# An attention and feed-forward kernel on one core: W_out's staging in a pool of its own, and three kinds of instruction in another place

## The chip, the cores and the metric

One core of a Trainium2 chip runs the whole program. Five engines work beside each other, each with its own list of instructions that it takes in order: TensorE (PE, with its weight loads as PEld), VectorE (DVE), ScalarE (ACT), GpSimd (POOL) and SyncE (SP), which issues the transfers. The metric is the device time of one execution in microseconds, the median of several.

## The reference

Eight batches of eight heads with 576 positions of 64 features go through attention with a block-causal mask (blocks of 64), then all 4608 tokens through a feed-forward layer with 512 in, 2048 hidden and 512 out.

```python
scores = scale * np.matmul(q, k.transpose(0, 1, 3, 2))      # scale = 1/8
scores = np.where(block_i >= block_j, scores, -1e9)
scores = scores - np.max(scores, axis=-1, keepdims=True)
attn = np.exp(scores)
attn = attn / (np.sum(attn, axis=-1, keepdims=True) + 1e-09)
x = np.matmul(attn, v)                                      # to (4608, 512)
h = x @ w_in
return ((h / (1 + np.exp(-h))) @ w_out).astype(np.float32)
```

## The kernel before, in words

The first two query blocks of each head are treated by special code at the start (`First`, `Second`). The other 448 query positions of each head are the main loop: 64 heads, called units u0 to u63, taken as 32 pairs d0 to d31, the even head in the upper half of the array's rows and the odd head in the lower half. The order of everything is written out by hand: `ORDER` is a long string of tokens such as `u36.max:0`, and the loop at L1258 calls the named method for each token. What a token emits goes to the end of its engine's list, so the table sets the order on each engine, and an engine waits at an instruction whose input is late.

For one pair, the steps are these.

- `dN.run:0` and `dN.run:1` (L793, matmuls at L802) are two runs of matmuls. Run 0 interleaves the scores of the even head with half of the product with v of the pair two earlier (tile `U`); run 1 does the same for the odd head (tile `u`). Scores lie in three PSUM banks for each head: x, y and z (names `S`, `S` and `SC` for the even head, `S`, `S` and `U` for the odd one).
- `max:0..2` (DVE, L663) takes block maxima of z, x and y into `Mx`; `ones` (ACT, L719) moves some of them across partitions; the end of `max:2` reduces them to `mj` (L715). `gather` (three ACT copies, L672), `top` (DVE, L727 and L729), `spread` (three ACT copies, L733) and `wide` (DVE, L667) bring the maximum of each row to where it is subtracted (`MR`). `sub:0..2` (DVE, L741 and L744) read the scores out of PSUM, which frees the banks, and `exp:0..2` (ACT, L748) follow.
- `add:0..3` (POOL, L755 to L763) add up the exponentials into `pa`, and `sums` (DVE, L663, tile `dj`) makes the row sums of it, once for each head. `sums_g` (three ACT copies), `sums_m` (POOL, L818 to L822) and `inverse` (DVE, L826 and L667) make the reciprocals.
- `half` (ACT, L806) and `fold` (DVE, L809) bring the product with v together, `mult` (POOL, L831) multiplies with the reciprocals, `x_hi` (ACT, L836) and `x_lo` (POOL, L839) split the result into two parts for the feed-forward layer.

The first feed-forward matmuls fill PE between the runs: each token `ffn` is six matmuls (L1077), two tokens fill a bank `h`, `keep` (ACT, L1083) copies it out to SBUF, which frees the bank, and `save` (SP) stores it to DRAM. There are two such banks, and the product `u` of each pair takes its turn in them too. Most pairs have eight `ffn` (48 matmuls of 448 columns); the pairs d2 to d5 and d9 have six (d2 to d4 with 512 columns, d5 with half of each).

Beside this, W_out is staged: 16 row blocks `o0` to `o15`, two for each of `t0` to `t7`. `load` brings 512 KB (tile `wst`), `rebias` (ACT, L540) and `bits:0..2` (DVE, L563, L567, L573) turn the 64-bit numbers into 32-bit ones in the tile `wraw`, and `hi` (ACT), `lo` and `x` (POOL for t0 to t3) make the split parts and differences for the second layer. t0 to t3 go into the pool `ta`, and t4 to t6 into a pool that exists only after the token `all.attended`, which releases the loop's pool:

```python
def attended(u):
    pools["work"].release()
    pools["work"] = tc.alloc_tile_pool(name="end", bufs=1, reuse_waits="tile")
```

The tiles of the staging (`os0`, `os1`, `wraw`) come from `pools["work"]` too, so those of before the token and those of behind it are different tiles. Behind the token stand o8 to o15, 42 `ffn` without attention, and then the second layer (items i0 to i71, L1160), which runs to the end.

Of the kernel before, what the change touches and what calls it, by code (L numbers as in the profile page):

```python
# [101 lines left out]
u1.exp:2 save u0.add:1 ffn u1.sub:1 u1.exp:0 u0.add:2 o2.bits:1 u1.exp:1 u0.add:3 o2.bits:2 d1.run:0 keep u1.add:0 u0.sums
o3.rebias save o3.bits:0 u1.add:1 o3.bits:1 u1.add:2 ffn u6.load u2.max:0 u7.load u1.add:3 u2.max:1 u2.ones ffn u2.max:2
u3.max:0 u2.gather ffn u3.ones u2.top keep u3.max:1 u2.spread u3.max:2 save ffn u2.wide u3.gather u2.sub:0 ffn keep u3.top
u2.sub:1 u3.spread save u1.sums u2.exp:0 ffn u2.sub:2 d0.sums_g u3.wide u2.exp:1 d0.sums_m ffn u3.sub:2 u2.exp:2 keep u3.sub:0
u3.exp:2 u3.sub:1 u2.add:0 save ffn d0.inverse u3.exp:0 u3.exp:1 u2.add:1 o3.bits:2 d2.run:0 keep u2.add:2 t1.hi:0 u2.add:3 save
t1.hi:1 u3.add:0 u2.sums d2.run:1 d0.half u4.max:0 u3.add:1 u4.max:1 u4.ones u3.add:2 u4.max:2 u3.add:3 u4.gather ffn u4.load_v
d0.fold t1.lo:0 u5.load_v u8.load u9.load u5.max:0 u4.top ffn d0.mult u5.ones u5.max:1 u4.spread u5.max:2 t1.lo:1 d0.x_hi ffn
u4.wide keep u4.sub:0 u5.gather d0.x_lo save ffn u4.exp:0 u5.top u4.sub:1 t1.x:0 u5.spread u3.sums ffn u4.exp:1 u4.sub:2 keep
u4.add:0 u5.wide d1.sums_g save ffn u5.sub:2 u4.exp:2 d1.sums_m t1.hi:2 u5.sub:0 u5.exp:2 u5.sub:1 d3.run:0 u4.add:1 keep  # L110
d1.inverse u5.exp:0 save u4.add:2 u5.exp:1 u4.add:3 d3.run:1 u5.add:0 d1.half u4.sums u6.max:0 u5.add:1 u6.max:1 u6.ones
u6.max:2 u5.add:2 ffn u5.add:3 u6.load_v u7.load_v d1.fold u10.load u11.load u6.gather u7.max:0 d1.mult ffn u6.top u7.ones
u7.max:1 u6.spread t1.lo:2 u7.max:2 d1.x_hi ffn u6.wide keep d1.x_lo u7.gather u6.sub:0 save ffn t1.x:1 u7.top u6.exp:0 u6.sub:1
u7.spread u5.sums t1.x:2 ffn u6.exp:1 u6.sub:2 keep u7.wide u6.add:0 d2.sums_g save ffn u7.sub:2 u6.exp:2 d2.sums_m u7.sub:0
u7.exp:2 u7.sub:1 d4.run:0 u7.exp:0 keep u6.add:1 d2.inverse u7.exp:1 save u6.add:2 t1.hi:3 u6.add:3 d4.run:1 d2.half u7.add:0
u6.sums u8.max:0 u7.add:1 u8.max:1 u8.ones u8.max:2 ffn u7.add:2 u8.load_v u9.load_v u12.load u7.add:3 u13.load d2.fold
u8.gather u9.max:0 ffn d2.mult u8.top u9.ones u9.max:1 u8.spread t1.lo:3 u9.max:2 ffn keep u8.wide u9.gather save ffn u8.sub:0
d2.x_hi u9.top u8.exp:0 d2.x_lo u8.sub:1 u9.spread u7.sums ffn keep u8.sub:2 d3.sums_g save u9.wide ffn u8.exp:1 d3.sums_m
u9.sub:2 u8.exp:2 u9.sub:0 u9.exp:2 d5.run:0 u9.sub:1 keep u8.add:0 d3.inverse u9.exp:0 save u9.exp:1 u8.add:1 u8.add:2 d5.run:1
d3.half u8.add:3 u9.add:0 u8.sums u10.max:0 ffn u9.add:1 u10.max:1 u10.load_v u10.ones u11.load_v u14.load u15.load u10.max:2  # L120
u9.add:2 u9.add:3 ffn d3.fold u10.gather u11.max:0 d3.mult u10.top u11.ones ffn u11.max:1 keep u11.max:2 u10.spread save ffn
u11.gather u10.wide d3.x_hi u10.sub:0 d3.x_lo u11.top u10.exp:0 u10.sub:1 u11.spread u9.sums u10.exp:1 ffn u10.sub:2 d4.sums_g
u10.add:0 u11.wide u10.exp:2 ffn u11.sub:2 keep d4.sums_m u11.sub:0 u11.exp:2 save d6.run:0 u11.sub:1 keep u11.exp:0 u10.add:1
save d4.inverse u11.exp:1 u10.add:2 u10.add:3 d6.run:1 d4.half u11.add:0 u10.sums u12.max:0 u11.add:1 u12.max:1 u12.ones ffn
u12.max:2 u11.add:2 u12.load_v u13.load_v u16.load u17.load u11.add:3 d4.fold u12.gather ffn u13.max:0 d4.mult u12.top u13.ones
u13.max:1 ffn u12.spread u13.max:2 keep u12.wide ffn d4.x_hi save u13.gather d4.x_lo u12.sub:0 ffn u13.top keep u12.sub:1
u13.spread save u11.sums ffn u12.exp:0 u12.sub:2 d5.sums_g u13.wide ffn u12.exp:1 d5.sums_m u13.sub:2 keep u13.sub:0 u12.exp:2
save ffn u13.sub:1 u13.exp:0 u12.add:0 d5.inverse u13.exp:1 d7.run:0 u13.exp:2 u12.add:1 keep u12.add:2 save u12.add:3 d7.run:1
u13.add:0 d5.half u12.sums u14.max:0 u13.add:1 u14.max:1 u14.ones u14.max:2 u13.add:2 ffn u13.add:3 u14.load_v u15.load_v
d5.fold u18.load u19.load u14.gather u15.max:0 d5.mult ffn u14.top u15.ones u15.max:1 u14.spread ffn u15.max:2 keep u14.wide  # L130
d5.x_hi save ffn u15.gather d5.x_lo u14.sub:0 u15.top u14.exp:0 ffn u14.sub:1 keep u13.sums u15.spread save u14.sub:2 ffn
d6.sums_g u15.wide u14.exp:1 d6.sums_m u15.sub:2 ffn u14.exp:2 u15.sub:0 keep u15.exp:2 u15.sub:1 u14.add:0 save ffn d6.inverse
u15.exp:0 u15.exp:1 u14.add:1 d8.run:0 keep u14.add:2 save u14.add:3 u15.add:0 u14.sums d8.run:1 d6.half u16.max:0 u15.add:1
u16.max:1 u16.ones u16.max:2 u15.add:2 u15.add:3 ffn u16.gather u16.load_v d6.fold u17.load_v u20.load u21.load u17.max:0
d6.mult ffn u16.top u17.ones u17.max:1 u16.spread u17.max:2 ffn keep u16.wide u17.gather save ffn u16.sub:0 d6.x_hi u17.top
u16.exp:0 d6.x_lo u16.sub:1 ffn u17.spread u15.sums keep u16.sub:2 d7.sums_g ffn save u17.wide u16.exp:1 d7.sums_m u17.sub:2
u16.exp:2 ffn u17.sub:0 keep u17.sub:1 u17.exp:0 u16.add:0 save ffn d7.inverse u17.exp:1 u17.exp:2 u16.add:1 d9.run:0 keep
u16.add:2 save u16.add:3 u17.add:0 u16.sums d9.run:1 d7.half u18.max:0 u17.add:1 u18.max:1 u18.ones u17.add:2 u18.max:2
u17.add:3 u18.gather ffn u18.load_v d7.fold u19.load_v u22.load u23.load u19.max:0 d7.mult ffn u18.top u19.ones u19.max:1
u18.spread u19.max:2 ffn keep u18.wide u19.gather save ffn u18.sub:0 d7.x_hi u19.top u18.exp:0 d7.x_lo u18.sub:1 u19.spread  # L140
u17.sums keep u18.sub:2 ffn d8.sums_g save u19.wide u18.exp:1 d8.sums_m u19.sub:2 ffn u18.exp:2 u19.sub:0 u19.exp:2 u19.sub:1
d10.run:0 u19.exp:0 u18.add:0 d8.inverse keep u19.exp:1 save u18.add:1 u18.add:2 d10.run:1 u18.add:3 d8.half u19.add:0 u18.sums
u20.max:0 u19.add:1 u20.max:1 ffn u20.ones u20.load_v u21.load_v u24.load u25.load u20.max:2 u19.add:2 u19.add:3 ffn d8.fold
u20.gather u21.max:0 d8.mult ffn u20.top u21.ones u21.max:1 keep u21.max:2 u20.spread save ffn d8.x_hi u20.wide u21.gather
d8.x_lo ffn u20.sub:0 keep u21.top u20.exp:0 u20.sub:1 save ffn u21.spread u19.sums u20.sub:2 d9.sums_g ffn u21.wide keep
d9.sums_m u20.exp:1 u21.sub:2 save ffn u20.exp:2 u21.sub:0 u21.exp:2 u20.add:0 u21.sub:1 u21.exp:0 d11.run:0 d9.inverse keep
u20.add:1 u21.exp:1 save u20.add:2 u20.add:3 d11.run:1 d9.half u21.add:0 u20.sums u22.max:0 u21.add:1 u22.max:1 u22.ones
u22.max:2 u21.add:2 ffn u22.load_v u23.load_v u26.load u21.add:3 u27.load d9.fold u22.gather ffn u23.max:0 d9.mult u22.top
u23.ones u23.max:1 ffn u22.spread u23.max:2 keep u22.wide d9.x_hi ffn save u23.gather d9.x_lo u22.sub:0 ffn u23.top u22.exp:0
u22.sub:1 keep u21.sums u23.spread save ffn u22.sub:2 d10.sums_g u23.wide u22.exp:1 ffn d10.sums_m u23.sub:2 keep u22.exp:2  # L150
u23.sub:0 save ffn u23.exp:2 u23.sub:1 u22.add:0 d10.inverse u23.exp:0 u23.exp:1 d12.run:0 u22.add:1 keep u22.add:2 save
u22.add:3 u23.add:0 d12.run:1 u22.sums d10.half u24.max:0 u23.add:1 u24.max:1 u24.ones u24.max:2 u23.add:2 ffn u23.add:3
# [1158 lines left out]
```

## Time and profile before

| | |
|---|---|
| median of 3 runs | 962.75 us (962.7 to 963.15) |
| the profiled execution's own time | 963.81 us |
| its span, first to last instruction | 962.1 us |
| mean granted TensorE clock | 1.000 |
| PE busy / PEld busy | 98% / 86% |
| DVE / ACT / POOL busy | 76% / 67% / 58% |

The profiled execution is some 1.1 us longer than the median of the runs, and 1.7 us of it lie outside the span. Busy shares are over the whole span. The ends of matmuls are modelled, and one overlaps the next, so that a busy PE may still start its matmuls late: starts are what to compare.

### The profile page before, as it was taken

The page shows a single profiled execution, that of the slowest core. Times are in us where ns is not written, and L with a number is a line of the kernel's source. Part 1 is how long each engine was busy: PE and PEld are TensorE (multiplying, and loading weights), DVE is VectorE, ACT ScalarE, POOL GpSimd, SP SyncE. Part 2 cuts the span into 40 slices and gives each one's busy share as a digit, 9 for nine tenths or more (in the row PEclk, how much of TensorE's full clock was granted, in tenths as well). Part 3 has the DMA queues.
Part 4 walks back from the last instruction along what each step waited for, and adds up shares of the span by engine and source line. Part 5 has one row for each costly group of instructions (what it writes and reads, how often), then busy time and mean ns, then how long its engine had stood idle before and what let it go on. Part 6 is the DMA issues. An engine that isn't in the chain of part 4 may idle for free.

```text
span 962.1 us, 23795 instructions
## 1 busy us (share of the span) xinstructions
PE 945.1 (98%) x8730; PEld 823.9 (86%) x8730; DVE 735.1 (76%) x1515; ACT 641.4 (67%) x1621; POOL 558.9 (58%) x803
## 2 busy tenths in 40 slices
...
GB/s 354 389 161 178 117 105 125 124 112 126 133 105 133 116 175 122 105 133 166 115 128 110 89 112 235 201 153 155 154 162 146 111 162 139 139 124 152 143 67 44
DMA packets 109813, 139.97 MB, mean 145 GB/s; under 512 B 22656, under 2 KB 87168, under 8 KB 109696
## 3 DMA queue, kind: packets, MB, share of 16 engines
...
## 4 chain that ended last, share of the span: by engine, by line
PE 46%; DVE 20%; POOL 17%; ACT 8%; issue 5%; DMA 2%; SPq 0%; POOLq 0%; DVEq 0%; ACTq 0%
PE c L1160 20%; PE S L1160 16%; DVE Mx L663 9%; PE h L1077 8%; POOL pa L758 4%; POOL pa L755 4%; POOL pa L763 3%; POOL rs L822 3%; DVE dj L663 2%; ACT m L733 2%; ACT g L1083 2%; DVE MR L667 2%; ACT dj L672 2%; DVE xu L809 2%; DVE p L741 2%
## 5 line engine op out<-in xcount | busy, mean ns | idle before, releaser
L1077 PE MATMUL h<-x,wi 128*128 128x448 f32 (+2 forms) x1968 | 417.5, 368 | 7.9 <-ACT g L1083 4.2
L1077 PEld LDWEIGHTS h<-x,wi 128*128 128x128 f32 x1968 | 356.1, 188 | 53.4 <-ACT g L1083 11.6
L1142 POOL TENSOR_TENSOR wi<-raw,wi 128x512 fp32r<-128x512 f32 (+1 forms) x114 | 115.8, 1031 | 148.6 <-ACT wi L1138 107.9
L748 ACT ACTIVATE p<-p 128x448 f32<-128x448 f32 (+2 forms) x192 | 100.9, 571 | 5.3 <-DVE p L741 1.6
L802 PE MATMUL S<-qk 64*64 64x384 f32 (+1 forms) x512 | 99.2, 517 | 0.0
L1083 ACT COPY g<-h 128x448 f32<-128x448 f32 (+1 forms) x160 | 85.7, 536 | 20.1 <-PE h L1077 14.8
L663 DVE TRANSPOSE_TENSOR_REDUCE dj<-pa 128x14 f32<-128x448 f32 x64 | 40.6, 634 | 73.5 <-POOL pa L763 73.5
L1160 PE MATMUL c<-ta,wi 128*128 128x256 f32 x684 | 87.0, 276 | 0.0
L1105 ACT ACTIVATE raw<-raw 128x1024 f32<-128x1024 f32 x72 | 76.7, 1065 | 13.7 <-DMA raw<-gdb 9.9
L758 POOL TENSOR_TENSOR pa<-pa,p 128x256 f32<-128x256 f32 (+1 forms) x128 | 79.1, 618 | 10.0
L755 POOL TENSOR_TENSOR pa<-p 128x448 f32<-128x448 f32 x64 | 73.2, 1143 | 15.8 <-ACT p L748 10.9
L1160 PEld LDWEIGHTS c<-ta,wi 128*128 128x128 f32 x684 | 81.9, 188 | 0.0
L1160 PE MATMUL c<-tb,wi 128*128 128x256 f32 x498 | 81.4, 276 | 0.0
L802 PE MATMUL U<-p,v 64*64 64x64 f32 (+4 forms) x768 | 79.8, 354 | 0.8 <-DVE p L744 0.8
L719 ACT COPY Mx<-Mx 64x4 f32<-64x4 f32 x128 | 24.7, 193 | 81.4 <-DVE Mx L663 79.8
L802 PE MATMUL u<-p,v 64*64 64x64 f32 (+4 forms) x768 | 78.6, 351 | 0.0
L741 DVE TENSOR_TENSOR p<-S,MR 128x448 f32<-128x448 f32 (+1 forms) x128 | 71.6, 581 | 1.1
L1160 PEld LDWEIGHTS c<-tb,wi 128*128 128x128 f32 x498 | 71.0, 188 | 0.0
L1160 PE MATMUL S<-ta,wi 128*128 128x256 f32 x534 | 70.2, 276 | 0.0
L663 DVE TRANSPOSE_TENSOR_REDUCE Mx<-S 128x14 f32<-128x448 f32 (+1 forms) x128 | 69.2, 576 | 0.0
L802 PEld LDWEIGHTS u<-p,v 64*64 64x64 f32 x768 | 43.9, 133 | 28.2 <-issue 23.2
L1160 PEld LDWEIGHTS S<-ta,wi 128*128 128x128 f32 x534 | 65.0, 188 | 0.0
...
## 6 DMA issues: line engine op xcount, KB each, us to landing
gdb<-g SPq DMA_DIRECT2D x128, 224.0 KB, 1.9
...
```

Of the source, the lines that this page charges most:

```text
L663: nc.vector.tensor_reduce(out=out, in_=in_, axis=AX.X, op=op, apply_transpose=True)
L741: nc.vector.tensor_tensor(out=u.p[:, c : c + w], in0=s[:, :w], in1=u.mb[:, q : q + w], op=ALU.subtract)
L748: nc.scalar.activation(u.p[:, c : c + w], u.p[:, c : c + w], AF.Exp, scale=SCALE)
L755: nc.gpsimd.tensor_tensor(out=u.pa, in0=p[:, :NQ], in1=p[:, ZERO:COLS], op=ALU.add)
L758: nc.gpsimd.tensor_tensor(out=u.pa[:, q : q + w], in0=u.pa[:, q : q + w], in1=p[:, c : c + w], op=ALU.add)
L763: nc.gpsimd.tensor_tensor(out=o, in0=o, in1=s, op=ALU.add)
L802: nc.tensor.matmul(o, w, x, start=start, stop=stop)
L1077: nc.tensor.matmul(o, w, x, start=half == 0 and i == 0 or f is None and i == 0, stop=(half == 1 or f is None) and i == len(runs) - 1)
L1083: nc.scalar.copy(g, hs.pop(z)[:, :n])
L1105: nc.scalar.activation(u.raw, u.raw, AF.Silu)
L1142: e.tensor_tensor(out=u.goal(1, k), in0=u.source(k), in1=u.goal(0, k), op=ALU.subtract)
L1160: nc.tensor.matmul(o[:, :HD], *runs[k], start=first, stop=u.q == 3 and n == 5, skip_group_check=True)
```

## The change

The staging of W_out gets a pool `raw` of its own that lives through the whole program. With it, o8 and o9 no longer have to wait for `all.attended`: their `load` now stands at d27 and their `rebias` and `bits` at d28 to d30 (a step stands "at dN" when it comes behind `dN.run:0` and ahead of the next pair's). For t4 the first two steps of `bits` now write in place (`wraw`) and no longer into a PSUM bank. The other staging in the loop is placed anew: `rebias` and `bits` of o2 and o3 from d0 and d1 to d9 to d11, t1 from d2 to d4 to d11 to d14; o4 and o5 from d18 to d20 to d15 to d17, t2 from d21 to d24 to d17 to d21; o6 and o7 from d24 to d26 to d22 to d24, t3 from d26 to d29 to d24 to d27.

```diff
+    rp = pool("raw")
...
-                u.raw = sp.tile([P, 512], I64, tag=f"os{u.i}", name="wst")
+                u.raw = rp.tile([P, 512], I64, tag=f"os{u.i}", name="wst")
...
-                u.a = (bank("C") if u.kind == "in" or u.d >= NTA else u.w).bitcast(U32)
+                u.a = (bank("C") if u.kind == "in" or u.d > NTA else u.w).bitcast(U32)
...
-                u.w = sp.tile([P, 4, 256], F32, tag="wraw", name="wraw")
+                u.w = rp.tile([P, 4, 256], F32, tag="wraw", name="wraw")
...
-            u.raw = sp.tile([P, 2, 4, P], F32, tag=("os0", "os1", "wraw", "xs")[u.n % 4], name="raw")
+            u.raw = (sp if u.n % 4 == 3 else rp).tile([P, 2, 4, P], F32, tag=("os0", "os1", "wraw", "xs")[u.n % 4], name="raw")
```

The table holds the same 4472 tokens in another order. On PE nothing moves: its 2065 rows are the same ones in the same order (apart from the line numbers, which the new line shifts by one). In the loop, two things move in every pair.

On DVE, in the middle of the loop, these rows stand from the end of one pair's work to the z maxima of the next odd head. `dj` is the row sums of an even head, `Mx` from `SC` and the two `S` are the maxima of the next even head, `xu` is `fold`. Before:

```order
L663 TENSOR_REDUCE dj<-pa 128x14
L663 TENSOR_REDUCE Mx<-SC 128x2x8
L663 TENSOR_REDUCE Mx<-S_7692 128x14
L663 TENSOR_REDUCE Mx<-S_7693 128x12
L715 TENSOR_REDUCE mj<-Mx 128x14
L809 TENSOR_TENSOR xu<-u,xu 128x448
L663 TENSOR_REDUCE Mx<-U 128x2x8
```

The same place on DVE in the changed kernel:

```order
L664 TENSOR_REDUCE Mx<-SC 128x2x8
L664 TENSOR_REDUCE Mx<-S_7706 128x14
L664 TENSOR_REDUCE Mx<-S_7707 128x12
L716 TENSOR_REDUCE mj<-Mx 128x14
L810 TENSOR_TENSOR xu<-u,xu 128x448
L664 TENSOR_REDUCE dj<-pa 128x14
L664 TENSOR_REDUCE Mx<-U 128x2x8
```

The row sums have gone from ahead of the next even head's maxima to behind them and behind `fold`.

On ACT, one pair's rows from the first bank copy (`g<-h`, which is `keep`) to the last exponential of the odd head; `mj` is `gather`, `x` is `x_hi`, `m` is `spread` of the odd head, `p` the exponentials, `dj` is `sums_g`. Before:

```order
L1083 COPY g<-h 128x448
L672 COPY mj<-mj 32x14 x3
L836 CAST x<-xu 128x448
L748 ACTIVATE p<-p 128x448
L733 COPY m<-m 32x18 x3
L1083 COPY g<-h 128x448
L672 COPY dj<-dj 32x28 x3
L748 ACTIVATE p<-p 128x384
L748 ACTIVATE p<-p 128x512
L1083 COPY g<-h 128x448
```

The same place on ACT in the changed kernel:

```order
L1084 COPY g<-h 128x448
L837 CAST x<-xu 128x448
L673 COPY mj<-mj 32x14 x3
L1084 COPY g<-h 128x448
L734 COPY m<-m 32x18 x3
L749 ACTIVATE p<-p 128x448
L673 COPY dj<-dj 32x28 x3
L1084 COPY g<-h 128x448
L749 ACTIVATE p<-p 128x384
L749 ACTIVATE p<-p 128x512
```

The second and the third copy of a bank now stand ahead of an exponential that they stood behind, the second also ahead of `spread`, and `x_hi` stands ahead of the odd head's `gather`. The fourth copy moves likewise ahead of the odd head's last exponential.

On ACT behind the loop, from the last `half` (`xu<-U`) on; `wraw<-wst` is `rebias`, `tb` is `hi` of t4. Before:

```order
L806 COPY xu<-U 128x448
L1083 COPY g<-h 128x448
L836 CAST x<-xu 128x448
L1083 COPY g<-h 128x448 x2
L540 ACTIVATE wraw<-wst 128x512 x2
L1083 COPY g<-h 128x448
L651 CAST tb<-wraw 128x256
```

In the changed kernel:

```order
L807 COPY xu<-U 128x448
L1084 COPY g<-h 128x448
L837 CAST x<-xu 128x448
L1084 COPY g<-h 128x448 x3
L652 CAST tb<-wraw 128x256
```

The two `rebias` of o8 and o9 are gone from between the bank copies.

## Rows read from the trace of the kernel before

**Rows 1.** The page: the span, and busy time of each engine.

```profile
span 962.1 us, 23795 instructions
...
PE 945.1 (98%) x8730; PEld 823.9 (86%) x8730; DVE 735.1 (76%) x1515; ACT 641.4 (67%) x1621; POOL 558.9 (58%) x803
```

**Rows 2.** Waits of PEld, 100 to 580: total, times, longest.

```profile
PEld h L1077 <- ACT g L1083: 11.6, 22, 1.7
PEld h L1077 <- DVE xu L809: 5.7, 9, 1.0
...
PEld U L802 <- DVE p L744: 3.9, 5, 1.4
...
PEld h L1077 <- POOL x L839: 1.0, 1, 1.0
```

**Rows 3.** Timeline of PE, d11: start, time, line, instruction, count.

```profile
238.62 0.59 PE L802 MATMUL S<-qk 64*64 64x448 f32 x2
...
243.33 9.88 PE L1077 MATMUL h<-x,wi 128*128 128x448 f32 x48
...
253.15 0.59 PE L802 MATMUL S<-qk 64*64 64x448 f32 x2
```

**Rows 4.** Chain that ended last, behind the loop: start, time, piece.

```profile
577.14 38.68 PE h L1077 x192
```

**Rows 5.** Timeline of PE, first matmul of d2, of d9 and of d32.

```profile
107.74 0.59 PE L802 MATMUL S<-qk 64*64 64x448 f32 x2
...
209.86 0.59 PE L802 MATMUL S<-qk 64*64 64x448 f32 x2
...
553.13 0.59 PE L802 MATMUL u<-p,v 64*64 64x448 f32 x2
```

**Rows 6.** Timeline of PE, d10's run 0.

```profile
221.99 0.97 PE L802 MATMUL S<-qk 64*64 64x448 f32 x4
223.55 0.59 PE L802 MATMUL U<-p,v 64*64 64x448 f32 x2 [0.59 <-DVE p L744]
```

**Rows 7.** Timeline of PE, feed-forward matmuls of 512 columns.

```profile
66.88 5.79 PE L1077 MATMUL h<-x,wi 128*128 128x512 f32 x24
```

**Rows 8.** Timeline of a late pair; in brackets idle time before, and its end.

```profile
494.11 0.59 PE L802 MATMUL S<-qk 64*64 64x448 f32 x2
...
506.25 2.31 PEld L1077 LDWEIGHTS h<-x,wi 128*128 128x128 f32 x12 [0.32 <-ACT g L1083]
...
507.05 0.69 DVE L744 TENSOR_TENSOR p<-U,MR 128x512 f32<-128x512 f32 x1
...
508.87 0.59 PE L802 MATMUL S<-qk 64*64 64x448 f32 x2
...
511.19 0.54 PE L802 MATMUL u<-p,v 64*64 64x448 f32 x2
...
511.26 0.98 POOL L763 TENSOR_TENSOR pa<-pa,p 64x128 f32<-64x128 f32 x2
...
512.27 0.65 DVE L663 TRANSPOSE_TENSOR_REDUCE dj<-pa 128x14 f32<-128x448 f32 x1 [2.60 <-POOL pa L763]
...
512.84 0.67 DVE L663 TRANSPOSE_TENSOR_REDUCE Mx<-SC 128x16 f32<-128x512 f32 x1
```

**Rows 9.** DVE by form, 170 to 550: busy, mean ns, idle before.

```profile
L663 DVE TRANSPOSE_TENSOR_REDUCE dj<-pa 128x14 f32<-128x448 f32 x51 | 32.3, 634 | 57.7 <-POOL pa L763 57.7
...
L567 DVE SCALAR_TENSOR_TENSOR wraw<-wst,wraw 128x512 uint32<-128x512 uint32 x4 | 4.1, 1036 | 0.1
L573 DVE SCALAR_TENSOR_TENSOR wraw<-wst,wraw 128x512 uint32<-128x512 uint32 x4 | 3.6, 912 | 0.0
```

**Rows 10.** Timeline behind the loop, at o8 and o9.

```profile
576.00 0.66 ACT L540 ACTIVATE wraw<-wst 128x512 f32<-128x512 f32 x1 [1.34 <-DMA wst<-in_moe_w_out_dram]
...
577.14 15.08 PE L1077 MATMUL h<-x,wi 128*128 128x448 f32 x74 [1.32 <-ACT g L1083]
```

**Rows 11.** DVE by form, 570 to 620: the same step with a PSUM operand.

```profile
L567 DVE SCALAR_TENSOR_TENSOR SC<-wst,SC 128x512 uint32<-128x512 uint32 x8 | 5.6, 696 | 0.3
```

More of the change, by code (lines that the diff above doesn't have):

```diff
@@ L102 @@
[L102 to L152, printed above, removed]
-u24.load_v d10.fold u25.load_v u24.gather u28.load u29.load u25.max:0 d10.mult ffn u24.top u25.ones u25.max:1 u24.spread
@@ L184 @@
-u36.exp:2 ffn u37.sub:0 keep u37.sub:1 u37.exp:0 u36.add:0 save ffn d17.inverse u37.exp:1 u37.exp:2 o4.bits:0 u36.add:1
-d19.run:0 keep o4.bits:1 u36.add:2 save u36.add:3 u37.add:0 u36.sums d19.run:1 d17.half u38.max:0 u37.add:1 u38.max:1 u38.ones
-u37.add:2 u38.max:2 u37.add:3 o4.bits:2 u38.gather ffn u38.load_v u39.load_v u42.load d17.fold u43.load u39.max:0 d17.mult ffn
-u38.top u39.ones u39.max:1 u38.spread ffn u39.max:2 keep u38.wide d17.x_hi save ffn u39.gather d17.x_lo u38.sub:0 o5.rebias
@@ L293 @@
[L293 removed]
+c3.lo u3.load_v t0.hi:3 u2.load d0.run:0 keep u3.load save ffn u4.load u0.max:0 u5.load u0.max:1 u0.ones ffn u0.max:2 u1.max:0
+u0.gather ffn u1.ones u0.top keep u1.max:1 ffn u0.spread u1.max:2 save u0.wide u1.gather ffn u0.sub:0 keep u1.top u0.exp:0 save
+ffn u0.sub:1 u1.spread u0.sub:2 u0.exp:1 u1.wide ffn u0.add:0 keep u1.sub:2 u0.exp:2 save u1.sub:0 u1.exp:2 u0.add:1 ffn
@@ new lines @@
+o2.rebias u16.add:3 o2.bits:0 d9.run:1 u17.add:0 d7.half u18.max:0 u18.max:1 u18.ones u17.add:1 u18.max:2 u17.add:2 ffn
+u18.gather u17.add:3 u18.load_v d7.fold u19.load_v u22.load u23.load u16.sums d7.mult ffn u19.max:0 u18.top u19.ones u19.max:1
+ffn u18.spread u19.max:2 keep u18.wide d7.x_hi ffn save u19.gather d7.x_lo u18.sub:0 u19.top keep u18.sub:1 ffn u19.spread save
+u17.sums u18.exp:0 u18.sub:2 d8.sums_g ffn u19.wide u18.exp:1 d8.sums_m u19.sub:2 u19.sub:0 keep d10.run:0 u18.exp:2 u19.sub:1
@@ new lines @@
+d11.run:0 keep u20.add:1 u21.exp:0 o3.bits:0 save u21.exp:1 u20.add:2 o3.bits:1 u20.add:3 d11.run:1 d9.half u22.max:0 u21.add:0
+u22.max:1 u22.ones u22.max:2 u21.add:1 u21.add:2 o3.bits:2 u22.gather ffn u22.load_v u21.add:3 u23.load_v u26.load u27.load
+d9.fold t1.hi:0 u20.sums ffn t1.hi:1 d9.mult u23.max:0 u22.top ffn u23.ones u23.max:1 keep u23.max:2 u22.spread save ffn d9.x_hi
+u22.wide u23.gather d9.x_lo u22.sub:0 ffn keep u23.top u22.exp:0 u22.sub:1 save t1.lo:0 ffn u23.spread u21.sums u22.sub:2
@@ new lines @@
+u43.sub:1 u42.add:0 u43.exp:0 d20.inverse u43.exp:1 d22.run:0 keep u42.add:1 u43.exp:2 save u42.add:2 o6.rebias u42.add:3
+o6.bits:0 d22.run:1 u43.add:0 d20.half u44.max:0 u44.max:1 u44.ones u43.add:1 u44.max:2 u43.add:2 ffn u44.gather u43.add:3
+u44.load_v d20.fold u45.load_v u48.load u49.load u42.sums d20.mult ffn u45.max:0 u44.top u45.ones u45.max:1 ffn u44.spread
+u45.max:2 keep u44.wide d20.x_hi ffn save u45.gather d20.x_lo u44.sub:0 ffn u45.top keep u44.sub:1 u45.spread save u43.sums ffn
```

319 lines of the change are left out of this document (180 added, 139 removed).

## The prediction

> **What bounds the kernel now.** The page comes first: PE is busy for 945.1 of 962.1 us [rows 1], and since the change leaves PE's list as it is, only its waits can go or come. So the question is how late PE starts its matmuls, and which engine it then waits for.
>
> Next the timeline of PE through one pair, to find what a pair costs without a wait. At d11 the first matmul of run 0 starts at 238.62, the feed-forward matmuls at 243.33, the next pair's run 0 at 253.15 [rows 3]: 4.71 us for the two runs, 9.82 us for 48 matmuls, 14.53 us in all. Behind the loop 192 such matmuls take 38.68 us in one stretch [rows 4], 0.2015 us each, or 9.67 us for 48, so that 9.82 holds no wait worth the name. I call 14.53 the floor of a long pair.
>
> Then the loop as a whole. From d2's first matmul at 107.74 to d32's at 553.13 [rows 5] 30 pairs take 445.39 us, 25 long and 5 short ones. The short pair d9 takes 221.99 - 209.86 = 12.13 us [rows 5, 6]. For the short pairs with 512 columns, 24 matmuls take 5.79 us [rows 7], of which I take off 0.2 for the modelled end of the last; 36 then take 8.4 us, and with the runs 13.1 us. d5, half and half, is 12.6. The floor of the stretch is 25 x 14.53 + 12.13 + 3 x 13.1 + 12.6 = 427.3 us, and PE lost 18.1 us.
>
> The list of waits says to whom. From 100 to 580 PE's weight loads waited for the bank copies of ACT 11.6 us in 22 places, for `fold` on DVE 5.7 us in 9, for the last `sub` of an odd head, which frees the bank U, 3.9 us in 5, for `x_lo` 1.0 us once [rows 2]. These sum to 22.2 us, more than PE lost, because a weight load runs ahead of its matmul; they serve as shares, not as a sum.
>
> One late pair shows the two mechanisms. Run 0 starts at 494.11 and the next at 508.87, 14.76 us later; in between one weight load stood 0.32 us for a bank copy [rows 8]. And DVE stood 2.60 us at the row sums `dj` for POOL's last `add`, which ended at 512.24, while the even head's scores had been complete since 511.19 [rows 8]: the maxima behind `dj` started at 512.84, 1.65 us late. Over 170 to 550 this idle time is 57.7 us [rows 9]. It does not cost PE directly, but everything behind it on DVE is late: `fold` (which frees a bank), and the odd head's last `sub`, which ended at 507.74, 13.63 us after its pair's run 0 [rows 8], and is needed at 14.53.
>
> **The change, part by part.** *Row sums behind the maxima.* Nothing is added or removed. The maxima of the even head can start when run 0 ends, 2.32 us after its start, and not 3.97 us after it as now [rows 8]. The way from there to the end of the odd head's last `sub` is now 13.63 - 3.97 = 9.66 us. It becomes longer by the row sums, 0.63 us [rows 9], and by a wait of `fold` for the end of run 1 (4.71 after the start of run 0, where DVE comes some 2 us after 2.32), 0.4 us by estimate. U is then free at 2.32 + 9.66 + 0.63 + 0.4 = 13.0 us. The nearest measurement of that way, in a pair with no staging, is d9: U at 223.55 - 209.86 = 13.69 [rows 5, 6]. Between 13.0 and 13.69 I take 13.5, nearer the measured one, because ACT's copies now stand between DVE's steps in another order. The row sums themselves are needed some 5.4 us after run 0's start, and POOL's adds end 3.37 after it (512.24 - 508.87, [rows 8]), so that their wait is covered by 2 us. The bank U needs 14.53, so a long pair has 1 us to spare.
>
> *Bank copies ahead of exponentials.* The second copy is what the 0.32 us wait is for [rows 8]. It now stands ahead of `spread` and one exponential, more than a microsecond of ACT's work, and the wait of 0.23 us a pair (14.76 - 14.53) goes. What is late next is the odd head's exponentials and POOL's adds behind them, which are needed two pairs later for the product and 2 us later for the row sums; and the odd head's `gather`, which now stands behind `x_hi` and so behind POOL's `mult` (a rival, below).
>
> *Staging in the loop.* The same instructions stand in other pairs. A half costs DVE 1.04 + 0.91 us for two steps [rows 9], and for the first, which reads one tile, at most the 0.70 of a step with a PSUM operand [rows 11]: 2.65 us. At most three steps fall in one pair. From the freeing of U to the end of a pair's work DVE needs 1.93 us (507.74 to 512.27 - 2.60, [rows 8]), so it is done 13.5 + 1.93 = 15.4 us after run 0's start, and the next maxima start at 14.53 + 2.32 = 16.85. That gap of 1.4 us, the 0.4 ahead of `fold` and the 1 us at U take 2.8 us: all three steps, if none lies badly. I take 0.1 us for each of the 12 pairs with such steps, 1.2 us, between nothing and the 0.5 of half a step that finds no gap. o8 and o9 add 5.3 us of DVE and 1.3 of ACT (0.66 each, [rows 10]) to the loop, in these same gaps of d28 to d30; without that cover they would cost PE at most what they take, 6.6 us.
>
> *o8 and o9 out of the end.* There ACT stood 1.34 us at `rebias` for the transfer, with a bank copy behind it, and PE stood 1.32 us for that copy [rows 10]. The transfer now starts a pair ahead of its `rebias`. Gain 1.3 us. Adding a wait of about 0.4 us for `fold` in the tail of the loop, which stays, PE's losses behind 100 us are 18.1 + 1.3 + 0.4 = 19.8 us. That is the most that can be won.
>
> *What stays.* The short pairs are shorter than DVE's way to U. d2 to d4: 13.5 - 13.1 = 0.4 us each, 1.2. d5: 13.5 - 12.6 = 0.9, with the wait for `x_lo` of 1.0 [rows 2] in the same place: 1.0. d9: 13.5 - 12.13 = 1.4. The tail 0.4. Staging 1.2. Sum 5.2 us. Everything behind 577 stays, since PE has no wait there [rows 4].
>
> **The sum.** 19.8 - 5.2 = 14.6 us. The profiled execution's own time is 963.8 (a span of 962.1 and 1.7 around it), and becomes 949.2; the median of the runs shown is 1.1 us lower, so that I forecast 948.1.
>
> **A rule against it.** The in-place steps of `bits` read two tiles in SBUF; they took 1.04 and 0.91 us beside the loop's POOL work, and the same step with one operand in PSUM 0.70 [rows 9, 11], so 0.34 and 0.21 are lost to something. The Trainium skill, SBUF — State Buffer, "Who interferes with whom", says that a VectorE instruction with two SBUF inputs and a GpSimd instruction that reads SBUF exclude each other, and the second one waits until the first is done. The trace agrees in sign; the means do not show a full wait each time. The third rival is this.
>
> **The rivals.** *The way to U stays too long in long pairs.* `x_hi` now stands ahead of `gather` on ACT, and waits for `mult` on POOL; with POOL late, `gather`, `top`, `spread` and the odd head's last `sub` are late too. For it speaks that POOL's adds were the last to end in the late pair [rows 8]; against it, that `mult` has fewer steps ahead of it (t's `lo` and `x` stand behind it now). From 14.53 on, each excess is lost in each of 25 long pairs; with what is lost now, 0.23, this gives back 5.8 us: 953.9. If both DVE and POOL slip by another 0.1, 956.4.
>
> *No gain.* The waits change their names: PE waits for U or `fold` as much as it did for the bank copies. For it speaks that four different things end PE's waits now [rows 2], against it that the way is 1.65 us shorter at its head. Then 961 to 964.5.
>
> *Staging steps block each other.* Each of the 16 in-place steps in the loop is held by a whole add of POOL (0.49 for one of the smallest, [rows 8]) and holds POOL in turn; the 12 pairs with staging lose 0.5 us more each: 954.
>
> *Slower.* The row sums now stand between the even and the odd head's maxima, so a late `pa` no longer delays the next pair's start but the odd head, directly ahead of U. It decides when POOL's adds end later than the row sums' place (2 us of cover) and the 1 us at U together, 3 us later than now. To be slower than before by 1.9 us it must cost 14.6 + 1.9 = 16.5 us in 25 pairs, 0.66 each, that is POOL 3.7 us later in every pair: 964.6 or more. POOL is busy for 58% [rows 1]; I see no place for it, except in pairs with staging.
>
> *Stall-free.* U at 13.0, nothing lost to staging: only d5, d9 and the tail lose, 0.9 x 1 + 0.9 + 0.4 = 2.2, and it is 945.1.
>
> **How the numbers follow.** Forecast 0.58 (its own range 945.5 to 951.5); way to U 0.14 (951.5 to 957); staging 0.06 (951.5 to 956); stall-free 0.08 (944 to 945.5); no gain 0.08; slower 0.06. The likeliest gives 948.1. From 944.5 to 957 lies about 0.83 of it, and this is the range. A measurement of this kernel tells about 0.2% from no change, 1.9 us: faster 0.86, same 0.08, slower 0.06.
>
> **What would show it.** In the changed trace: DVE's wait at `dj` for POOL (57.7 us) nearly gone, and in its place a wait of the maxima for PE's scores; PE's weight loads waiting for bank copies 11.6 us down to 2 or less, for `fold` under 1.5; long pairs at 14.53 from run 0 to run 0, staging ones within 0.3 of it; a wait for U left in d9 and the early short pairs; no wait of `rebias` for the transfer behind the loop, and PE's last stretch of the first layer starting some 1.3 us sooner after the loop. Wrong would be the forecast if long pairs stay above 14.7, with PE waiting for U, or `top` on DVE waiting for `gather`.

## The result and the profile after

The changed kernel takes 946.44 us (median of 4 runs, 946.14 to 947.82), against 962.95 us for the kernel before beside it (4 runs, 962.7 to 964.34): a ratio of 0.9828, with a 95% interval of 0.9811 to 0.9845. The forecast was 948.1 us. The profiled execution takes 946.67 us, of which the span is 944.9. Its page answers to [rows 1]:

```profile
span 944.9 us, 23760 instructions
...
PE 935.7 (99%) x8730; PEld 824.7 (87%) x8730; DVE 738.4 (78%) x1515; ACT 643.3 (68%) x1621; POOL 558.8 (59%) x803
```

The waits of PE's weight loads from 100 to 580, as in [rows 2]; the columns are the total, the number and the longest:

```profile
PEld S L803 <- DVE rr L827: 4.3, 14, 0.3
...
PEld U L803 <- DVE p L745: 0.8, 1, 0.8
PEld h L1078 <- POOL x L840: 0.4, 1, 0.4
...
PEld h L1078 <- DVE xu L810: 0.2, 1, 0.2
```

No bank copy stands there any more, `fold` stands with 0.2 us, U with one place. The loads for `S`, at the head of a run, run ahead of their matmuls and cost nothing: PE's own list of waits is empty in this stretch. The timeline of PE at d2, d9, d10 and d32, and at the first matmul of the second layer:

```profile
108.07 0.59 PE L803 MATMUL S<-qk 64*64 64x448 f32 x2
...
204.30 0.59 PE L803 MATMUL S<-qk 64*64 64x448 f32 x2
...
216.43 0.97 PE L803 MATMUL S<-qk 64*64 64x448 f32 x4
...
217.44 0.59 PE L803 MATMUL U<-p,v 64*64 64x448 f32 x2
...
537.09 0.59 PE L803 MATMUL u<-p,v 64*64 64x448 f32 x2
...
597.57 0.40 PE L1161 MATMUL S<-ta,wi 128*128 128x256 f32 x2
```

And that first matmul in the timeline of the kernel before:

```profile
615.66 0.40 PE L1160 MATMUL S<-ta,wi 128*128 128x256 f32 x2
```

So the 17.2 us between the two spans lie as follows. From d2 to d32: 445.39 us before, 429.02 now, 16.4 gained. From d32 to the second layer: 62.53 before, 60.48 now, 2.05 gained. From there to the end of the span: 346.44 before, 347.33 now, 0.9 lost. And d2 starts 0.33 us later, which is scatter of the start (107.5 to 108.4 over the traces here, but for two kernels in which a bank copy holds PE ahead of d2, b_copies_early and b_both). Against the floor of 427.3 us the loop still loses 1.7: 1.0 in d10's run 0, where the product waits for U (217.44, and not some 216.45), 0.5 in d5 and d6, the rest in d2 to d4. From d11 to d31 the run 0s follow each other at 14.53 us, with staging and without.

One long pair, d24, in the timeline (PE, POOL, DVE and ACT), to set beside [rows 8]:

```profile
435.38 0.59 PE L803 MATMUL S<-qk 64*64 64x448 f32 x2
...
437.50 0.98 POOL L764 TENSOR_TENSOR pa<-pa,p 64x128 f32<-64x128 f32 x2
...
437.92 0.72 DVE L664 TRANSPOSE_TENSOR_REDUCE Mx<-SC 128x16 f32<-128x512 f32 x1 [1.97 <-PE U L803]
...
440.25 0.62 DVE L810 TENSOR_TENSOR xu<-u,xu 128x448 f32<-128x448 f32 x1 [0.24 <-PE u L803]
...
440.79 0.64 DVE L664 TRANSPOSE_TENSOR_REDUCE dj<-pa 128x14 f32<-128x448 f32 x1
...
445.21 0.53 ACT L1084 COPY g<-h 128x448 f32<-128x448 f32 x1 [0.35 <-PE h L1078]
...
447.79 0.69 DVE L745 TENSOR_TENSOR p<-U,MR 128x512 f32<-128x512 f32 x1
...
449.91 0.59 PE L803 MATMUL S<-qk 64*64 64x448 f32 x2
```

DVE now waits for PE and not for POOL: the maxima start 2.54 us after run 0 (3.97 before). `fold` waits 0.24 for the end of run 1. POOL's adds of the even head end at 438.48, the row sums want them at 440.79. The third bank copy behind run 0 (445.21; it is the second in the rows of the section on the change, and the one that PE waited for in [rows 8]) waits for PE's own matmuls. U is free at 448.48, 13.1 us after run 0 and 1.4 before it is needed.

### The profile page after: what moved, and what is told of

The parts are those of the page before. It is cut to its first block, busy times and chain, and to the rows that moved or that the text cites. A ratio compares the mean times of both kernels' runs of the same rounds, so it can differ in the third digit from the quotient of the medians.

```text
span 944.9 us, 23760 instructions
## 1 busy us (share of the span) xinstructions
PE 935.7 (99%) x8730; PEld 824.7 (87%) x8730; DVE 738.4 (78%) x1515; ACT 643.3 (68%) x1621; POOL 558.8 (59%) x803
## 3 DMA queue, kind: packets, MB, share of 16 engines
q8 instruction: 68, 1.11, 0.5%
## 4 chain that ended last, share of the span: by engine, by line
PE 95%; DVE 2%; ACT 1%; DMA 1%; SPq 0%; issue 0%; POOL 0%; DVEq 0%; ACTq 0%
PE h L1078 41%; PE c L1161 21%; PE S L1161 16%; PE u L803 7%; PE S L803 5%; PE SC L803 3%; PE U L803 1%; DMA p<-in_qk_dram 1%; PE S L1006 1%; PE S L882 1%; PE S L1047 0%; ACT MR L1020 0%; DVE Mx L664 0%; DVE dj L664 0%; ACT wi L583 0%
## 5 line engine op out<-in xcount | busy, mean ns | idle before, releaser
L1078 PE MATMUL h<-x,wi 128*128 128x448 f32 (+2 forms) x1968 | 410.0, 366 | 0.5 <-POOL wi L586 0.2
L1161 PE MATMUL S<-tb,wi 128*128 128x256 f32 x384 | 64.0, 276 | 0.0
```

Of the source, the lines that this page charges most:

```text
L1078: nc.tensor.matmul(o, w, x, start=half == 0 and i == 0 or f is None and i == 0, stop=(half == 1 or f is None) and i == len(runs) - 1)
L1161: nc.tensor.matmul(o[:, :HD], *runs[k], start=first, stop=u.q == 3 and n == 5, skip_group_check=True)
```

## The experiments

Names are those of the section on the change; L numbers shift by one or two between kernels. "Loop" is the start of d32 less that of d2 in the timeline, "behind" is from d32 to the first matmul of the second layer, "second layer" from there to the end of the span. Ratios are to the kernel before on the same chip.

| kernel | median us | ratio, 95% interval | loop | behind | second layer |
|---|---|---|---|---|---|
| before | 962.95 | 1 | 445.39 | 62.53 | 346.44 |
| changed | 946.44 | 0.9828 (0.9811 to 0.9845) | 429.02 | 60.48 | 347.33 |
| a_sums_back | 963.05 | 0.9999 (0.9990 to 1.0009) | 445.47 | 61.27 | 347.33 |
| a_copies_back | 947.30 | 0.9834 (0.9817 to 0.9850) | 430.74 | 60.59 | 347.39 |
| a_both_back | 971.91 | 1.0091 (1.0076 to 1.0106) | 455.01 | 60.70 | 346.28 |
| a_o89_at_end | 946.95 | 0.9835 (0.9820 to 0.9850) | 429.02 | 62.00 | 346.46 |
| b_sums_behind | 951.06 | 0.9869 (0.9854 to 0.9884) | 433.04 | 62.24 | 346.40 |
| b_copies_early | 959.23 | 0.9960 (0.9946 to 0.9974) | 439.84 | 61.77 | 346.23 |
| b_both | 954.64 | 0.9905 (0.9892 to 0.9920) | 434.26 | 62.18 | 346.44 |
| a_pause_short | 945.34 | 0.9812 (0.9798 to 0.9827) | 429.02 | 60.46 | 346.47 |
| a_room_1 | 947.40 | 0.9835 (0.9817 to 0.9853) | 430.69 | 60.48 | 346.23 |
| a_room_2 | 960.76 | 0.9970 (0.9960 to 0.9981) | 444.39 | 60.64 | 346.49 |
| a_sums_back_nobits | 953.92 | 0.9902 (0.9884 to 0.9921) | 436.81 | 61.19 | 346.41 |
| a_best | 946.04 | 0.9820 (0.9806 to 0.9833) | 429.79 | 60.46 | 346.39 |

**Undoing the change by parts.** The row sums back ahead of the maxima (the adds that they need go along; POOL's own order stays as in the changed kernel):

```diff
 d14.half
+u30.add:3 u30.sums
 u32.max:0
-u30.add:3
...
 d14.fold u31.add:1 u33.load_v u36.load u37.load
-u30.sums
 d14.mult
```

> The changed kernel with each even head's row sums put back ahead of the next even head's maxima on DVE (31 places); the order on PE, ACT and POOL stays. Theory (each of the two moves buys room at a place of its own, and a long pair has room to spare): DVE waits for POOL's last add again, some 1.2 us a pair, but the fold no longer waits for the end of run 1 and the row sums are gone from between the two maxima, so U comes free only about 0.35 us later; long pairs stay at 14.53 us, d6 and d10 lose 0.35 us each, fold waits once or twice: 946.5 to 948. Rival 1 (the prediction's weight: the late maxima are what PE paid for): waits for U and for fold come back in most long pairs, 14.6 to 14.75 us each: 949 to 952. Rival 2 (the new places of the staging alone bring the gain): no change at all, 946.4.

Measured: 963.05 us. The whole gain is gone, 16.5 us in the loop, more than any of the theories gave it. PE's weight loads wait for `fold` again, 13.6 us where the changed kernel has 0.2:

```profile
PEld h L1078 <- DVE xu L810: 13.6, 17, 1.4
```

DVE by form from 170 to 550 shows the wait of [rows 9] again:

```profile
L664 DVE TRANSPOSE_TENSOR_REDUCE dj<-pa 128x14 f32<-128x448 f32 x51 | 32.4, 634 | 51.7 <-POOL pa L764 51.7
...
L664 DVE TRANSPOSE_TENSOR_REDUCE Mx<-SC 128x16 f32<-128x512 f32 x26 | 17.5, 674 | 0.0
```

In the changed kernel the same two rows, and those of two staging steps, read:

```profile
L664 DVE TRANSPOSE_TENSOR_REDUCE dj<-pa 128x14 f32<-128x448 f32 x53 | 33.3, 628 | 3.4 <-POOL pa L764 3.4
...
L664 DVE TRANSPOSE_TENSOR_REDUCE Mx<-SC 128x16 f32<-128x512 f32 x25 | 17.9, 714 | 27.2 <-PE U L803 26.8
...
L574 DVE SCALAR_TENSOR_TENSOR wraw<-wst,wraw 128x512 uint32<-128x512 uint32 x8 | 7.5, 937 | 0.2
L568 DVE SCALAR_TENSOR_TENSOR wraw<-wst,wraw 128x512 uint32<-128x512 uint32 x8 | 7.1, 890 | 0.1
```

Where the 16.5 us lie says more than the sum. Long pairs without staging kept their 14.53 to 14.59 us, as the theory said; the loss is in the short pairs (d4 14.79, d5 15.81 where 13.17 and 12.81 stood) and in the long pairs with staging (d10 17.86, d11 15.79, d16 15.86). The timeline of d16, which starts at 313.96:

```profile
316.21 0.89 DVE L574 SCALAR_TENSOR_TENSOR wraw<-wst,wraw 128x512 uint32<-128x512 uint32 x1
...
318.19 0.97 POOL L764 TENSOR_TENSOR pa<-pa,p 64x128 f32<-64x128 f32 x2
...
319.20 0.65 DVE L664 TRANSPOSE_TENSOR_REDUCE dj<-pa 128x14 f32<-128x448 f32 x1 [2.09 <-POOL pa L764]
...
321.73 0.61 DVE L810 TENSOR_TENSOR xu<-u,xu 128x448 f32<-128x448 f32 x1
...
322.40 7.49 PE L1078 MATMUL h<-x,wi 128*128 128x448 f32 x36 [1.04 <-DVE xu L810]
```

POOL, late in this pair, ends its last add at 319.16; DVE stands 2.09 us at `dj`; `fold` ends at 322.34, and PE stands 1.04 for the bank. The row sums are back, but POOL's adds are later than they were in the kernel before: even in d14, a pair without `bits`, `dj` ends 4.54 us after run 0, and 4.05 before. So the 16.5 us are not the price of the row sums' place alone.

The bank copies back behind the exponentials:

```diff
-keep u30.add:0 u31.exp:0 save d14.inverse u31.exp:1 u31.exp:2
+u30.add:0 u31.exp:0 d14.inverse u31.exp:1 u31.exp:2 keep save
...
-keep u32.sub:1 u33.spread save u31.sums ffn u32.exp:0
+u32.sub:1 u33.spread u31.sums ffn u32.exp:0 keep save
...
-keep u33.sub:2 u32.exp:1 save u33.sub:0 u32.exp:2
+u33.sub:2 u32.exp:1 u33.sub:0 u32.exp:2 keep save
```

> The changed kernel with the second, third and fourth bank copies of each pair put back behind the exponentials that they stood behind (73 places on ACT). Theory: the third bank copy is late again for the seventh group of feed-forward matmuls, and a long pair takes 14.6 to 14.76 us: 2 to 6 us in 25 pairs, 948.5 to 952.5, with PE's weight loads waiting for bank copies in most pairs. Rival 1 (the row sums' move makes ACT's chain early enough for the copies in either place): long pairs at 14.53, 946.4 to 947.4. Rival 2 (staging alone): 946.4.

Measured: 947.30 us, not told from the changed kernel by the runs, 1.7 us longer in the loop by the trace. Rival 1 held: plain long pairs stay at 14.53 to 14.55; only d17, d24, d29 and d30, which have staging, lose 0.3 to 0.5 us each.

Both edits together:

> The changed kernel with row sums and bank copies both put back, so that what is left of the change is the pool, the new places of the staging, and o8 and o9 in the loop. Theory (the two moves bring the larger part, staging and the end some 4 to 6 us): 953 to 958, long pairs at 14.7 to 14.9 us. Rival (staging alone brings the gain, in that it had stood in the short pairs, which have no room): 946.4 to 949.

Measured: 971.91 us, 9 us slower than the kernel before. What is left of the change is a loss by itself while row sums and copies stand as before. It is not the staging's new places alone: d31, which has no staging, takes 14.96 us, and 14.76 before. `x_hi` still stands ahead of the odd head's `gather` here; ACT then stands 0.66 us at `spread`, and the third bank copy ends 12.3 us after run 0 and not 12.1. In d27, whose run 0 starts at 485.93:

```profile
496.57 0.64 ACT L733 COPY m<-m 32x18 f32<-32x18 f32 x3 [0.66 <-DVE m L729]
...
497.72 0.51 ACT L1083 COPY g<-h 128x448 f32<-128x448 f32 x1
```

How the 9 us divide between this and the staging was not tried. In the loop the copies, worth 1.7 us with the row sums behind, are worth 9.5 with them in front; the waits of the weight loads are those of [rows 2], larger:

```profile
PEld h L1077 <- ACT g L1083: 15.8, 21, 1.3
PEld h L1077 <- DVE xu L809: 10.0, 15, 1.8
```

**Doing the parts alone, on the kernel before.** The row sums behind `fold`:

```diff
-u30.sums d16.run:1 d14.half u32.max:0
+d16.run:1 d14.half u32.max:0
...
 d14.fold
+u30.sums
```

> The kernel before with one thing changed: each even head's row sums stand behind the next fold, as in the changed kernel (30 places on DVE). Theory now (the place of the row sums is what decides: behind the maxima DVE's wait for POOL's last add falls in time that DVE has, and staging is absorbed; the copies matter only where DVE's chain is late): long pairs at 14.53 to 14.6, what is left is the staging in the short pairs and in its old places: 948 to 953. Rival (the two moves need each other, and the 16.5 us that putting the sums back cost came from the changed kernel's later adds on POOL): PE's waits for bank copies stay, 956 to 961.

Measured: 951.06 us, as the theory said. Every pair from d11 to d24 and from d27 to d31 takes 14.53 us, with the bank copies at their old, late places and with staging in d18 to d20. The waits of the weight loads in that kernel:

```profile
PEld h L1077 <- ACT g L1083: 3.3, 4, 1.7
PEld U L802 <- DVE p L744: 2.4, 4, 1.0
```

Against [rows 2] the bank copies fall from 11.6 to 3.3 us, though none of them was moved. The third copy of d28, in the kernel before (run 0 at 494.11) and in this one (run 0 at 482.64):

```profile
505.67 0.53 ACT L1083 COPY g<-h 128x448 f32<-128x448 f32 x1
```

```profile
493.66 0.53 ACT L1083 COPY g<-h 128x448 f32<-128x448 f32 x1
```

It ended 12.09 us after run 0 and now ends 11.55 us after it: the maxima, on which ACT's steps ahead of the copy wait, start 2.54 us after run 0 and not 3.97. What this kernel lacks to the changed one, 433.04 - 429.02 = 4.0 us of loop, is in d2 to d6, where staging stands in it (13.94, 14.37, 13.57, 13.36 and 15.09 us, against 13.17 three times, 12.81 and 14.86: 3.1 us), and in d25 and d26 (0.9).

The copies alone:

```diff
 u33.top
+keep
 u32.exp:0 d14.x_lo u32.sub:1 ffn u33.spread u31.sums
-keep
...
 u33.wide
+keep
 u32.exp:1
...
 u33.exp:1
+keep
 u33.exp:2
```

> The kernel before with one thing changed: the third, fourth and first bank copies of a pair stand ahead of the exponentials that they stood behind (71 places on ACT). Theory now: the 0.23 us of the pairs without staging go (14.76 to 14.53), but DVE still waits for POOL at the row sums, so fold and U stay late in pairs with staging: 956 to 960, waits for bank copies below 4 us, waits for fold and U as before or more. Rival 1 (the copies alone carry the gain of long pairs): 948 to 953. Rival 2 (nothing, the later exponentials give back on POOL what the copies win): 962 to 964.

Measured: 959.23 us. As the theory said, the plain long pairs fall to 14.53, pairs with staging do not (d20 15.16, d25 17.25), and the waits for `fold` (5.2 us) and U (3.7) stay as large as in [rows 2].

Both, with the old staging and pools:

> The kernel before with both moves and its own staging and pools. Theory now: long pairs at 14.53 also with staging; what the changed kernel has beyond it is the staging taken out of the short pairs d0 to d4, and o8 and o9: 947.5 to 951. Rival (the new places of the staging carry a share of their own): 952 to 956.

Measured: 954.64 us, neither: slower than the row sums alone. The loop is 1.2 us longer (in d25, 16.69 us against 15.03), and d2 starts at 109.01 and not 107.72, because PE stands for a bank copy ahead of it, as it does in b_copies_early:

```profile
103.30 5.78 PE L1076 MATMUL h<-x,wi 128*128 128x512 f32 x24 [0.98 <-ACT g L1082]
```

So the copies' move is no gain by itself behind the row sums; where staging stands badly it costs.

**The end of the first layer.** The steps of o8 and o9 are taken out of d27 to d30 and stand again where they stood:

```diff
 all.attended
+o8.load o9.load
...
+o8.rebias
 ffn
+o8.bits:0 o9.rebias
...
```

> The changed kernel with load, rebias and bits of o8 and o9 back behind the loop, at the places of the kernel before. Theory (PE stood for the bank copy behind rebias, which waited for the transfer): the stretch from the last attention run to the second layer grows by 1.3 to 2 us, and the time is 947.7 to 948.4. Rival 1 (the tiles of the new pool are free early, so the transfer no longer comes late): below 0.4 us, 946.4 to 946.8. Rival 2 (o8 and o9 cost the loop something in d28 to d30): 946 or less. Beside it, the first 250 matmuls of the second layer in the changed kernel start 118 ns apart instead of 113; if what stands beside them on ACT and DVE causes it, it should move with the end's work, if not, it stays.

Measured: 946.95 us, not told from the changed kernel. The stall is there as in [rows 10], in the timeline behind the loop:

```profile
558.87 0.69 ACT L541 ACTIVATE wraw<-wst 128x512 f32<-128x512 f32 x1 [1.44 <-DMA wst<-in_moe_w_out_dram]
...
560.02 1.28 PE L1078 MATMUL h<-x,wi 128*128 128x448 f32 x5 [1.25 <-ACT g L1084]
```

"Behind" grows by 1.5 us, as the theory said; but the second layer is 0.9 shorter in this kernel's trace than in the changed kernel's, so that the time hardly moves, and the theory's 947.7 is missed. PE by form from 601 to 625, in the changed kernel:

```profile
L1161 PE MATMUL c<-ta,wi 128*128 128x256 f32 x45 | 5.9, 279 | 0.0
```

and in this one:

```profile
L1161 PE MATMUL c<-ta,wi 128*128 128x256 f32 x48 | 6.2, 277 | 0.0
```

The same kind of matmul takes 279 or 277 ns in the record, and more of them start in the same time. One edit was made to see whether a pause of PE brings that:

```diff
-keep t4.lo:1 t4.hi:2 t4.x:1 save ffn
+t4.lo:1 t4.hi:2 t4.x:1 ffn
 t4.x:2 t4.lo:2 t4.hi:3 ffn o10.rebias
+keep save
 t4.lo:3 keep
```

> The changed kernel with one bank copy behind the loop put off until after o10's rebias, so that PE pauses there for some 0.3 to 0.5 us. The two kernels that had a pause of about 1.3 us behind the loop went over from 118 to 113 ns between matmuls some 40 matmuls into the second layer, the three without it only after 247, and these 208 matmuls took 0.93 us longer. Theory (a pause of PE is what brings the early change): the second layer becomes 0.93 us shorter and the time 945.8 to 946.1, less than the changed kernel by 0.5 us. Rival 1 (only a long pause does it): the pause is lost, 946.7 to 947. Rival 2 (it is the work of o8 and o9 at this place, not the pause): the same as rival 1 here; a longer pause without o8 and o9 tells these apart.

Measured: 945.34 us; the second layer is 0.9 us shorter, but PE did not pause: the late copy was still in time, and PE's matmuls behind the loop follow each other as in the changed kernel. Over all the kernels the second layer takes 347.3 to 347.4 us in three, 346.2 to 346.5 in the rest, and the shorter one comes with a stall behind the loop (a_o89_at_end, b_copies_early) and without (a_pause_short, a_room_1, a_both_back). The theory of the pause falls.

**How much room there is.** The odd head's `wide` once or twice more, from d10 on (2 in this edit, 3 in the one for a_room_2):

```diff
-            bcast(u.mb, u.m[:, 0], NQX)
+            for _ in range(2 if u.e and u.i >= 20 else 1):
+                bcast(u.mb, u.m[:, 0], NQX)
```

> The changed kernel with the odd head's widening of the maxima (0.77 us on DVE, ahead of the last sub on U) done twice in pairs d10 to d31; it writes the same values again. Theory (U comes free 13.14 us after its pair's run 0 in a pair without staging, 13.5 in the pair with three staging steps that was looked at, and is needed at 14.53, so that there are 1.0 to 1.4 us of room): 22 pairs with 0.77 us more, and long pairs stay at 14.53; 946.2 to 947.5, loop 429 to 430 us, although DVE is busy for 17 us more. Rival (the room is used up in pairs with staging): 0.3 to 0.5 us in 12 pairs, 950 to 952.

Measured: 947.40 us, loop 430.69. All plain pairs stay at 14.53; d12, d16, d17, d18 and d31, behind staging, lose 0.14 to 0.53 us, 1.7 together.

> The same, with the widening done three times (1.54 us more). Theory: the room of 1.0 to 1.4 us is passed; each of the 22 pairs loses 0.15 to 0.55 us at U: loop 433 to 441 us, 950 to 958. Rival (it is POOL or ACT that ends last, and DVE has more room than U shows): 946 to 948.

Measured: 960.76 us, loop 444.39: 13.7 us for the second repetition, where the first took 1.7. The list of waits of the weight loads, and in the timeline the run 0s of d27 and d28, pairs without staging, with d27's first matmul into U:

```profile
PEld U L804 <- DVE p L746: 10.7, 12, 1.7
```

```profile
475.77 0.59 PE L804 MATMUL S<-qk 64*64 64x448 f32 x2
476.00 0.59 PE L804 MATMUL U<-p,v 64*64 64x448 f32 x2
...
490.52 0.59 PE L804 MATMUL S<-qk 64*64 64x448 f32 x2
```

Such a pair takes 14.75 us, 0.22 over the floor. One repetition moves the end of the last `sub` on U in d27 from 13.09 us after run 0 (changed) to 13.91 (a_room_1), which is 0.8 and a little more than `wide` itself; two add 1.6. The room at U in a pair without staging is then 1.6 - 0.2 = 1.4 us, and the way to U 14.53 - 1.4 = 13.1, as in d24 above; d10's wait in the changed kernel agrees (217.44 - 204.30 = 13.14, behind the short pair d9).

**Staging with the row sums in front.** The kernel with the row sums back, which here leaves out the steps `bits` of o2 to o9:

```diff
         def bits(u, j):
+            if u.kind == "out" and 1 <= u.d <= 4:
+                return
```

> The changed kernel with the row sums put back ahead of the maxima, and without the 24 steps of bits of o2 to o9 on DVE (that part of the computation is left out). With the row sums back the loop took 445.5 us, and the long pairs with staging 14.7 to 17.9, those without 14.53 to 14.59. Theory (DVE stands for POOL at the row sums while staging waits behind, so that staging is paid in full): without the steps the long pairs fall to 14.53 to 14.65, the short pairs d4 to d6 keep their loss of 4.6 us: loop 433 to 436 us, 951 to 954. Rival (the row sums' place costs by itself, whatever stands beside it): 958 or more.

Measured: 953.92 us, loop 436.81, as the theory said (0.8 more loop than its range). d11 falls from 15.79 to 14.53, d17 from 15.40 to 14.55, d30 from 15.42 to 14.53; d4 to d6 keep their loss. d16, d18 and d19 stay at 15.0 to 15.1: something beside these steps costs there, and which was not tried.

**A shorter way to U in the short pair.**

```diff
-o2.bits:0 d9.run:1
+d9.run:1
...
-u17.sums u18.exp:0 u18.sub:2 d8.sums_g ffn u19.wide u18.exp:1 d8.sums_m u19.sub:2
+u18.exp:0 u18.sub:2 ffn u19.wide u18.exp:1 u19.sub:2 u17.sums d8.sums_g d8.sums_m
 u19.sub:0 keep d10.run:0 u18.exp:2 u19.sub:1
+o2.bits:0
```

> The changed kernel with the put-off bank copy behind the loop (which took 945.34) and, in the short pair d9, the odd head's row sums (0.62 us) behind the last sub on U and one staging step (0.63 us) behind the odd head's subs. Theory (U ends last in the short pair): U comes free some 0.6 to 0.7 us sooner, the wait in d10's run 0 falls from 1.0 to 0.3 to 0.4 us: 944.6 to 945. Rival (the inverse and the staging steps, now later on DVE, delay d10's maxima and give it back): 945.3 or more.

Measured: 946.04 us; the rival held. DVE's timeline behind d10's run 0, which starts at 216.11:

```profile
215.86 0.69 DVE L745 TENSOR_TENSOR p<-U,MR 128x512 f32<-128x512 f32 x1
216.47 0.63 DVE L664 TRANSPOSE_TENSOR_REDUCE dj<-pa 128x14 f32<-128x448 f32 x1
...
219.72 0.24 DVE L827 RECIPROCAL rr<-rs 128x14 f32<-128x14 f32 x1 [1.26 <-POOL rs L823]
...
221.38 0.70 DVE L664 TRANSPOSE_TENSOR_REDUCE Mx<-SC 128x16 f32<-128x512 f32 x1
```

U is free at 216.55, 0.5 us sooner after its pair's start, but DVE then stands 1.26 us at the reciprocal for POOL, and d10's maxima start 5.27 us after its run 0. d10 takes 15.96 us (15.53 in the changed kernel), d11 14.81.

## Why the prediction was right, and where its terms were off

- **What bounds the kernel.** Right. PE's list did not change, and the floor of 14.53 us for a long pair is what d11 to d31 now take.
- **The row sums.** The mechanism was right, the wait of 57.7 us at `dj` became one of the maxima for PE's scores, and without it nothing is gained: put back, the time is that of before. Done alone, it brings 12.4 of the loop's 16.4 us. Its share is no fixed number, though: with the copies already early in the kernel before it is 5.6 us (b_copies_early to b_both), and taken out of the changed kernel 16.5. The working gave 13.0 us for the way to U, and 13.5 was taken, for the nearness to a measured row. 13.1 was measured: the row taken for nearest, d9's 13.69, was one of the kernel before, whose late maxima are in it.
- **The bank copies.** This is the step that failed. The wait of 0.23 us a pair was booked to the copies' new place. It went as well with the copies at their old place and the row sums behind (b_sums_behind), since ACT's steps wait for the maxima and those start sooner: the copy ends 0.54 us earlier after run 0, more than the 0.32 us that PE's load waited for it. Either edit alone ends the wait in plain long pairs; the copies' own share behind the row sums is 1.7 us of loop in the changed kernel, and -1.2 in the kernel before, with 1.3 us more lost ahead of d2.
- **Staging.** The 1.2 us for the 12 pairs measured 0: from d11 on U comes free 13.7 us after run 0 at the latest (in d11), and is needed at 14.53. What has no step of its own in the working, only a part in the 18.1 us lost, is the other side of the move, the short pairs that staging leaves: d2 to d6 gained 3.1 us over b_sums_behind. "What stays" had given d2 to d4 a loss of 1.2 us to a way of 13.5; with 13.1 they stand at 13.17. So what stays in the loop is 1.7 us and not 4.8 (the 5.2 without the tail).
- **A rule against it.** The in-place steps still take 890 and 937 ns in the mean, against 696 with a PSUM operand [rows 11]. By the Trainium skill, SBUF — State Buffer, "Who interferes with whom", such a step and a GpSimd instruction that reads SBUF exclude each other. The prediction saw no full wait in the means; single steps of the changed kernel show it, as the one at 406.80 in the timeline, which begins while an add of POOL runs to 407.15:

```profile
406.00 1.15 POOL L756 TENSOR_TENSOR pa<-p 128x448 f32<-128x448 f32 x1
...
406.80 0.89 DVE L568 SCALAR_TENSOR_TENSOR wraw<-wst,wraw 128x512 uint32<-128x512 uint32 x1
```

  It ends 0.54 us behind that add. All 16 in the loop end 0.54 to 0.58 us behind the POOL instruction that ran when they began, and take 0.65 to 1.11 us, by how much of it was left; the mean hides this. But the third rival that was built on it fell, because the pairs have room for it. In a_room_1 the room at U is 0.8 us smaller, and five pairs behind staging lose 1.7 us together.
- **The end.** 1.3 us was booked for o8 and o9; the stall is worth 1.5 by a_o89_at_end. With the tail of the loop, 2.05 came. "Everything behind 577 stays" was wrong by 0.9 us, in the second layer, for a reason that stays open.
- **The sum.** 14.6 us were forecast for the span. The loop and what lies behind it up to the second layer brought 18.4, 3.8 more: 3.1 in the loop, where 4.8 was to stay and 1.7 did, and 0.7 behind it; the second layer and the start took 1.2 back, which leaves the 17.2 us between the spans. The median misses by 1.7 us only, where the span's gain missed by 2.6, since it lies 0.2 us below the profiled execution and not 1.1. In the loop it is the stall-free rival that held: U at 13.0, nothing lost to staging, 1.8 us lost in d5 and d9. That the time lies in the forecast's own range, and not in that rival's, comes from the 1.2 us of the second layer and the start, which nothing in the working foresaw; so far the number was luck.

The slower rival wanted POOL's adds to end 3 us later, so that the row sums at their new place wait for them. They end 2.3 us ahead of it (438.48 against 440.79), and `dj` waited in one place, 3.4 us, in the tail.
